# Turning the second head's chunks round in each block of v, scores and kept keys, so that the products with v address all four quarters of TensorE's array

## The chip, the cores and the metric

One core of a Trainium2 chip runs the whole kernel. The metric is the device time of one execution in microseconds (us), given as the median of several fast runs with their lowest and highest. "PEclk" in a profile is the TensorE clock that was granted, as a fraction of full speed.

## The reference, cut to what matters

A gated linear attention over 4 batches and 8 heads (768 steps, head size 48) is followed by a low-rank mixer and a feed-forward layer (384 to 1536 to 384). All in fp32.

```python
def _attn_ref(q, k, v, f_logit):            # B, H, S, D = 4, 8, 768, 48
    f = 1.0 / (1.0 + np.exp(-f_logit))
    for t in range(S):
        state = f[:, :, t, :, None] * state + np.einsum('bhd,bhe->bhde', k[:, :, t], v[:, :, t])
        y[:, :, t] = np.einsum('bhd,bhde->bhe', q[:, :, t], state)
# x = y as (B, S, H*D)
def _moe_ref(x, U, V, w_ch1, w_ch2):
    h = x.transpose(0, 2, 1) @ U @ V
    u = x + h.transpose(0, 2, 1)
    return u + np.maximum(u @ w_ch1, 0.0) @ w_ch2
```

## The kernel before

The attention goes in 16 units, each a pair of heads (`par` 0 and 1). The sequence is cut into 6 blocks of 128 steps, each of two chunks of 64 (`s` 0 and 1). Within a chunk the scores are a 64x64 triangle, and across chunks a state is carried by a scan on VectorE. A unit's work on TensorE is: kept keys (transposes), states (`ds`), scores (`sc`), products of the states with q (`y` from `st`) and products of the scores with v (`y` from `v_nat`). Between these pieces the mixer of the batch before is laid in, which is most of TensorE's work (`pz`, `pw`, `po`). For the first four units there is no mixer yet.

`part[s]` is the lower or upper 64 partitions. It is the key to the change: the partitions of the operands choose the row half of the array, and the partitions of the output choose the column half (the prediction below names the page that says so). A quarter is one row half with one column half.

```python
    # load of v: a block of 128 steps on 128 partitions, so chunk s on part[s]
    v_tiles[n] = three.tile([P, NBL, 2, D], F32, name="v_nat")
    nc.sync.dma_start(out=dst[:, :, par, 0:D], in_=head.rearrange("(c p) d -> p c d", p=P))
    # ... (cut)
        part = [slice(s * C, (s + 1) * C) for s in range(2)]          # C = 64
        def scores():       # rows: the head's half; columns: the chunk's half
            # ... loops over c (blocks), par, s
                        nc.tensor.matmul(
                            sc[part[s], par, c * C : (c + 1) * C],
                            lhsT=T["k"][rows[par], chunk[2 * c + s]],
                            rhs=T["q"][rows[par], chunk[2 * c + s]],
                            start=True, stop=True)
            # ... VectorE: A = sc * causal mask
        def kept():         # the keys turned back, chunk s on part[s]
            # ...
                    nc.tensor.transpose(pt[:, par, c * PAD : (c + 1) * PAD],
                                        T["k"][r, c * P : (c + 1) * P], ident[r, r])
        def states():       # rows: the chunk's half; columns: the head's half
            # ...
                        nc.tensor.matmul(
                            ds[par * PAD : (par + 1) * PAD, s, c * D : (c + 1) * D],
                            lhsT=T["kb"][part[s], par, c, :], rhs=vt[part[s], c, par, :],
                            start=True, stop=True)
            # ... ScalarE copies ds; a scan on VectorE gives st[e, c], chunks innermost
            T["st"] = st.rearrange("p (e c) -> p c e", c=NCH)         # NCH = 12
        def read():         # y from st: rows: the head's half; columns: the chunk's half
            # ... rhs=T["st"][rows[par], c, :]   (48 elements, 12 apart)
        def inner():        # y from v: rows AND columns are the chunk's half
            # ... loops over reversed c, par, s
                        nc.tensor.matmul(
                            o(s, par, c),                             # y[part[s], par, ...]
                            lhsT=T["A"][part[s], par, c, :], rhs=vt[part[s], c, par, :],
                            start=False, stop=True, skip_group_check=True)
```

In `inner` only the two quarters on the diagonal, (0,0) and (1,1), are ever addressed.

## Time and profile before

| | before |
|---|---|
| time, median of 3 | 548.32 us (547.5 to 548.93) |
| span of the profiled run (548.67 us) | 546.9 us |
| TensorE busy | 94% of the span |
| first product of the feed-forward layer (`pz`) starts | 72.84 us |
| from there to the end | 474.0 us |

The last two rows split the kernel into an early part (loads, conversion of weights, the first four units, the first mixer's start, with many waits) and a late part in which TensorE hardly stops. This is the clock row of the profile page, the span in 40 equal slices of 13.7 us, each digit the granted clock in tenths:

```profile
PEclk9697599999999799999999999999999999999998
```

The reader is to see the second to fifth slices (14 to 68 us) at 6, 9, 7, 5, and one 7 in the slice from 178 us. The individual clock records say that TensorE ran at exactly half clock from 18.4 to 28.6, 42.3 to 45.7 and 52.5 to 66.1 us, which is 27.3 us in all before the first `pz`.

From the chain that ended last, in order of time, these are pieces that serve as milestones (start in us, us on the chain, what):

```profile
72.84 46.86 PE pz L167 x216
...
215.66 7.97 PE pz L167 x36
...
286.32 8.00 PE pw L212 x48
...
336.27 7.97 PE pz L167 x36
...
394.23 5.38 PE pz L167 x24
...
453.66 23.58 PE pz L167 x108
...
527.85 13.66 PE pw L212 x84
```

Every one of them is TensorE's.

### The profile page before, as it was taken

Reading aid. Unit: us, or ns where it says so; the run is one execution under the profiler, and the core shown is the slowest. Engines: PE = TensorE matmul, PEld = TensorE weight load, DVE = VectorE, ACT = ScalarE, POOL = GpSimd, SP = SyncE. Lnnn points to the kernel's source line nnn. Section 1 sums busy time; section 2 is a strip of 40 time slices with the busy share of each in tenths; the row PEclk is TensorE's granted clock in tenths of the full one; section 3 lists DMA queues with packets and bytes.
Section 4 is the critical chain, followed back from the end, with each engine's and each line's share of the span. In section 5 each row is a group of like instructions: output and inputs, shape, how many; then the busy total and the mean of one; then the engine's idle time right before and its main releaser. Section 6 shows DMA issues by size and latency. Waiting matters only on the chain.

```text
span 546.9 us, 11966 instructions
## 1 busy us (share of the span) xinstructions
PE 511.6 (94%) x5277; PEld 425.3 (78%) x5277; DVE 268.7 (49%) x406; ACT 145.6 (27%) x293; POOL 33.4 (6%) x47
## 2 busy tenths in 40 slices
PE   4676889999998999999999999999999999999996
PEld 3565478886775546889889877899899877898995
DVE  5675475556666866457485740645403340222231
ACT  3243365562222113322331213221321103202010
POOL 3001243341000000000000000000000000000000
PEclk9697599999999799999999999999999999999998
DMA  9988915523546335050805522010000000000001
GB/s 149 165 163 188 225 48 159 160 80 83 106 77 88 51 65 81 1 73 12 121 3 90 71 28 44 1 24 30 2 2 31 1 16 15 1 15 15 0 30 35
DMA packets 149077, 34.88 MB, mean 64 GB/s; under 512 B 139544, under 2 KB 147224, under 8 KB 149016
## 3 DMA queue, kind: packets, MB, share of 16 engines
q1 hardware_dynamic: 149016, 34.03, 32.9%
q8 instruction: 43, 0.70, 0.6%
q14 instruction: 18, 0.15, 0.1%
HBM read 29.29 MB, written 4.72 MB: 62 GB/s over the span
## 4 chain that ended last, share of the span: by engine, by line
PE 86%; DVE 5%; SPq 2%; DMA 2%; ACT 2%; issue 1%; DVEq 0%; ACTq 0%
PE pz L167 35%; PE pw L212 23%; PE po L189 9%; PE y L613 5%; PE y L595 4%; PE pt L454 3%; SPq L359 2%; PE ds L567 2%; PE sc L534 2%; PE pu L148 1%; PE pt L553 1%; PE ph L136 1%; DMA f_raw<-in_f_logit_dram 1%; PE put L157 1%; DMA v_nat<-in_v_dram 1%
## 5 line engine op out<-in xcount | busy, mean ns | idle before, releaser
L167 PE MATMUL pz<-uT,w 128*128 128x256 f32 x864 | 192.8, 382 | 0.7 <-ACT uT L159 0.7
L167 PEld LDWEIGHTS pz<-uT,w 128*128 128x128 f32 x864 | 162.3, 190 | 23.6 <-ACT uT L159 0.6
L174 ACT ACTIVATE z<-pz 128x512 f32<-128x512 f32 x63 | 37.7, 598 | 128.5 <-PE pz L167 124.4
L212 PE MATMUL pw<-w,z 128*128 128x192 f32 x324 | 56.2, 328 | 0.0
L212 PE MATMUL pw<-zw,w_raw 128*128 128x192 f32 x324 | 56.2, 328 | 0.0
L212 PEld LDWEIGHTS pw<-w,z 128*128 128x128 f32 x324 | 53.0, 190 | 1.4 <-DVE x L144 0.5
L212 PEld LDWEIGHTS pw<-zw,w_raw 128*128 128x128 f32 x324 | 52.8, 190 | 1.5 <-DVE o L144 1.2
L144 DVE TENSOR_TENSOR w_raw<-z 128x768 f32<-128x768 f32 x18 | 17.2, 953 | 58.6 <-ACT z L174 58.5
L486 DVE TENSOR_TENSOR_SCAN X<-fz,ends 128x768 f32<-128x768 f32 x16 | 28.1, 1753 | 20.6 <-ACT fz L475 14.4
L580 DVE TENSOR_TENSOR_SCAN st<-added,whole 128x576 f32<-128x576 f32 x16 | 21.6, 1352 | 29.6 <-ACT added L573 29.6
L613 PEld LDWEIGHTS y<-v_nat,A 64*64 64x64 f32 x768 | 26.8, 149 | 5.9 <-issue 5.1
L595 PE MATMUL y<-st,qT 48*64 48x48 f32 x704 | 20.8, 271 | 10.1 <-DVE st L580 10.1
L613 PE MATMUL y<-v_nat,A 64*64 64x48 f32 x768 | 28.8, 234 | 0.5 <-ACT seen L602 0.5
L595 PEld LDWEIGHTS y<-st,qT 48*64 48x64 f32 x704 | 18.0, 164 | 14.5 <-issue 12.0
L503 DVE TENSOR_TENSOR_SCAN Y<-fz,starts 128x768 f32<-128x768 f32 x16 | 28.0, 1749 | 0.2
L68 POOL TENSOR_TENSOR w<-w_y,w_r 128x384 int32<-128x384 int32 x24 | 25.4, 1057 | 42.1 <-DVE w_y L67 40.8
L189 PE MATMUL po<-w,zw 128*128 128x384 f32 x72 | 27.2, 524 | 0.0
L189 PE MATMUL po<-w,z 128*128 128x384 f32 x72 | 25.2, 493 | 0.0
L65 DVE TENSOR_SCALAR w_y<-w_y 128x384 f32<-128x384 f32 (+1 forms) x27 | 11.1, 409 | 28.3 <-ACT w_y L63 28.3
L148 PE MATMUL pu<-h,V 128*128 128x384 f32 x48 | 21.3, 566 | 2.0 <-DVE x L144 0.7
L144 DVE TENSOR_TENSOR w_y<-x,pw 128x192 f32<-128x192 f32 x9 | 3.2, 355 | 39.3 <-ACT w_y L225 39.3
L144 DVE TENSOR_TENSOR w_y<-w_y,pw 128x192 f32<-128x192 f32 x18 | 6.3, 351 | 31.3 <-PE pw L212 31.3
(91 smaller groups left out, 510.9 us busy)
## 6 DMA issues: line engine op xcount, KB each, us to landing
w_raw<-in_moe_w_ch_dram SPq DMA_DIRECT2D x18, 384.0 KB, 3.1
v_nat<-in_v_dram SPq DMA_DIRECT2D x32, 144.0 KB, 3.5
out_dram<-o SPq DMA_DIRECT2D x24, 192.0 KB, 2.0
f_raw<-in_f_logit_dram SPq DMA_DIRECT2D x16, 144.0 KB, 2.9
k_raw<-in_k_dram SPq DMA_DIRECT2D x16, 144.0 KB, 4.2
q_raw<-in_q_dram SPq DMA_DIRECT2D x16, 144.0 KB, 4.2
zw<-in_moe_w_ch_dram SPq DMA_DIRECT2D x6, 384.0 KB, 14.5
f_raw<-in_f_logit_dram SPq DMA_DIRECT2D x16, 96.0 KB, 3.2
```

What stands on the lines that cost most here:

```text
L68: nc.gpsimd.tensor_tensor(dst.bitcast(I32), shaped(y.bitcast(I32)), shaped(r), ALU.add)
L144: nc.vector.tensor_tensor(*args)
L148: nc.tensor.matmul(pm[:, 0:DM], lhsT=V[:, t * P : (t + 1) * P], rhs=h[0], start=True, stop=True)
L167: nc.tensor.matmul(pm[:, i * 2 * P : (i + 1) * 2 * P], lhsT=w1[:, m, o : o + P], rhs=uT[a][:, m, :], start=(m == 0), stop=(m == NDC - 1))
L174: nc.scalar.activation(z[a, c][:, k : k + 2, :].rearrange("p i t -> p (i t)"), pm, AF.Relu)
L189: nc.tensor.matmul(pm, lhsT=z[a, i // NI][:, i % NI, s * P : (s + 1) * P], rhs=w2[:, i, :], start=(i == 0), stop=(i == NFC - 1))
L212: nc.tensor.matmul(pm[:, n * HM : (n + 1) * HM], lhsT=lhs[:, i, :], rhs=rhs[:, i, :], start=(i == 0), stop=(i == NI - 1))
L486: nc.vector.tensor_tensor_scan(backwards(X, S - 1, S), backwards(f, S, S), backwards(ends, S - 1, S), 0.0, ALU.mult, ALU.add,)
L503: nc.vector.tensor_tensor_scan(Y, f[:, 0:S], starts, 0.0, ALU.mult, ALU.add)
L580: nc.vector.tensor_tensor_scan(st, added[:, 0 : D * NCH], whole.rearrange("p e c -> p (e c)"), 0.0, ALU.add, ALU.mult)
L595: nc.tensor.matmul(o(c % 2, par, c // 2), lhsT=T["q"][rows[par], chunk[c]], rhs=T["st"][rows[par], c, :], start=(c <= 2), stop=False, skip ...
L613: nc.tensor.matmul(o(s, par, c), lhsT=T["A"][part[s], par, c, :], rhs=vt[part[s], c, par, :], start=False, stop=True, skip_group_check=True,)
```

## The change

The intent is to let the products with v use four quarters. For the second head (`par` 1) the two chunks of each block change places in v, in the scores and in the kept keys, while y keeps its places. So `inner` takes the operands of the second head from `part[s ^ 1]` and writes `part[s]`: quarters (1,0) and (0,1) beside the first head's (0,0) and (1,1). The states and scores keep using four quarters in another order. v's second head needs two loads of 64 partitions instead of one of 128. The kept keys of the second head are read 64 columns further left, so the key tile gets 64 zero columns in front and a fixed place. With that shift the second chunk of a block lies in the next block of kept keys, which is the `i` of `states`; the last chunk finds the zeros there, and no later chunk reads its state.

```diff
@@ load
+                if nm == "v" and par:
+                    for s in range(2):
+                        nc.sync.dma_start(
+                            out=v_tiles[n][(1 - s) * C : (2 - s) * C, :, par, :],
+                            in_=head.rearrange("(c s p) d -> s p c d", s=2, p=C)[s],
+                        )
+                    continue
@@ constants
+    kz = [const.tile([P, C + S], F32, name=f"kz{i}") for i in range(2)]
+    for i in range(2):
+        nc.gpsimd.memset(kz[i][:, 0:C], 0.0)
@@ operand
-            t = T[nm] = two.tile([P, S], F32, name=f"{nm}T")
+            t = T[nm] = kz[n % 2][:, C:] if nm == "k" else two.tile([P, S], F32, name="qT")
@@ scores
-                            sc[part[s], par, c * C : (c + 1) * C],
+                            sc[part[s ^ par], par, c * C : (c + 1) * C],
@@ kept
+                    o = c * P + (1 - par) * C
-                        pt[:, par, c * PAD : (c + 1) * PAD], T["k"][r, c * P : (c + 1) * P], ident[r, r]
+                        pt[:, par, c * PAD : (c + 1) * PAD], kz[n % 2][r, o : o + P], ident[r, r]
@@ states
+                        i = (c + (s & par)) % NBL
-                            lhsT=T["kb"][part[s], par, c, :], rhs=vt[part[s], c, par, :],
+                            lhsT=T["kb"][part[s ^ par], par, i, :], rhs=vt[part[s ^ par], c, par, :],
@@ inner
-                            o(s, par, c), lhsT=T["A"][part[s], par, c, :], rhs=vt[part[s], c, par, :],
+                            o(s, par, c), lhsT=T["A"][part[s ^ par], par, c, :], rhs=vt[part[s ^ par], c, par, :],
```

## The prediction

> **What bounds the kernel now.** I read the page's busy shares first, then the chain that ended last, then the chain piece by piece in order of time, then the groups of TensorE instructions.
>
> ```profile
> PE 511.6 (94%) x5277; PEld 425.3 (78%) x5277; DVE 268.7 (49%) x406; ACT 145.6 (27%) x293; POOL 33.4 (6%) x47
> ...
> PE 86%; DVE 5%; SPq 2%; DMA 2%; ACT 2%; issue 1%; DVEq 0%; ACTq 0%
> PE pz L167 35%; PE pw L212 23%; PE po L189 9%; PE y L613 5%; PE y L595 4%; PE pt L454 3%; SPq L359 2%; PE ds L567 2%; PE sc L534 2%; PE pu L148 1%; PE pt L553 1%; PE ph L136 1%; DMA f_raw<-in_f_logit_dram 1%; PE put L157 1%; DMA v_nat<-in_v_dram 1%
> ```
>
> The reader is to see that TensorE is busy for 94% of the span and carries 86% of the chain, so time taken off its stream is time off the end, except where something else sets the pace. The line under change, "PE y L613" (scores times v), has 5% of the chain. Going through the records for gaps in TensorE's work, I find about 25 us in all: nearly 18 us between its first instruction and 73 us, 3.5 us at 175.5 to 179.0, and the rest in pieces under 0.5 us around the mixer's additions and transposes. From 215 to 318 us there is none.
>
> Now one unit (one pair of heads) of the late part, from the chain in order of time:
>
> ```profile
> 294.31 0.84 PE ds L567 x48
> 295.16 2.15 PE pw L212 x12
> 297.31 0.86 PE sc L534 x48
> 298.17 5.38 PE pz L167 x24
> 303.54 1.17 PE y L595 x44
> 304.71 2.79 PE pz L167 x12
> 307.50 1.53 PE y L613 x48
> 309.03 4.10 PE pw L212 x24
> ```
>
> Columns: start us, us on the chain, what. Three groups have 48 instructions each on 64-column weights. The states (ds) take 0.84 us and the scores (sc) 0.86, but y L613 takes 1.53. The code says why: ds and sc touch all four quarters of the array, whereas y L613 has both its row half and its column half given by part[s], so only the two quarters on the diagonal. The groups view gives the same shapes:
>
> ```profile
> L613 PE MATMUL y<-v_nat,A 64*64 64x48 f32 x768 | 28.8, 234 | 0.5 <-ACT seen L602 0.5
> L595 PE MATMUL y<-st,qT 48*64 48x48 f32 x704 | 20.8, 271 | 10.1 <-DVE st L580 10.1
> L567 PE MATMUL ds<-v_nat,kb 64*64 64x48 f32 x768 | 14.9, 221 | 1.5 <-ACT kb L557 1.0 <-DMA v_nat<-in_v_dram 0.3
> L534 PE MATMUL sc<-qT,kT 48*64 48x64 f32 x768 | 14.5, 220 | 0.0
> ```
>
> y L613 is busy for 28.8 us, ds with the same form for 14.9. In the records one by one, ds and sc start in bursts of four, some 7 ns apart, one burst each 58 ns. y L613 starts in bursts of two, also one each 58 ns. So one quarter takes one instruction per 58 ns in all three groups, and y L613 leaves half of them empty.
>
> **What the Trainium skill says.** "TensorEngine Tiling (Array Packing)", Tile-to-Partition Mapping: in 64x64 mode there are four tiles, and rows of the operands and partitions of the output pick the tile. Its Key Properties: tiles work in parallel, and a change of tiling mode drains the engine. The trace agrees: bursts of four; and sc directly behind ds takes 0.71 us where it takes 0.86 behind a full-array product, so a switch costs about 0.15 us. The change leaves the number of switches alone. "TensorE: Matmul & The Clock Gate", LDWEIGHTS: a load takes the number of columns divided by 1.2, in ns: 53 for 64; the trace's 58 ns per instruction and quarter is near, so the weight load sets the rate of a quarter. The first page's Gotcha 1: different row tiles cannot use one PSUM bank at once. The trace doesn't show that as a loss: y L613 of before sends both row halves to one bank 7 ns apart at the full 58 ns rate. The clock page's Part 1: after idling, TensorE runs at half rate. Here the granted clock was 0.50 from 20 to 28 us and 0.68 from 54 to 73.
>
> **The change part by part.** The order of TensorE's instructions is the same in both kernels, with the same counts.
>
> Products with v (y L613): 24 products, 48 instructions, 16 units. Two quarters: 24 bursts of two, 24 x 58.3 = 1.40 us; measured from first load to last start 1.385 us. Four quarters: 12 bursts, 0.70 us, and ds with its same form measures 0.699. So 0.686 us less per unit. Late units (5th to 16th): eleven at full clock, 11 x 0.686 = 7.5; the eighth begins at half clock, 1.843 to about 0.93, 0.9 less. Sum 8.4 us. First four units: 2.50, 1.39, 1.73 and 2.50 us (two at half clock), halved: 1.2 + 0.7 + 0.9 + 1.2 = 4.0 us.
>
> States (ds): its quarters were all used, and are, in another order: now (row, column) halves (0,0), (1,1), (1,0), (0,1). No change. Scores: outputs of the second head swap halves, still four quarters, no change. Kept keys: 12 transposes of the same shape, shifted by 64 columns for the second head; no change. The key tile of fixed place stays doubled, by unit parity; no new wait.
>
> VectorE, ScalarE: the same work; from about 189 us on the scheduler orders some VectorE and ScalarE instructions otherwise. GpSimd: two 64-column clears, some 0.1 us each, behind those that the first transposes wait for.
>
> Loads: the second head of v comes in two loads of 64 partitions, 16 more issues, bytes and 192-byte packets the same. Only the start can feel it: issues are on the chain until f_raw of the third unit lands.
>
> ```profile
> 13.16 0.73 SPq L359
> 13.94 5.66 DMA f_raw<-in_f_logit_dram
> 19.60 0.14 issue
> 19.73 1.51 PE pt L454 x6
> ```
>
> Two more issues stand ahead of it (0.84 us each now), but an issue of 768 packets takes 0.84 us because the engines take packets at about 0.9 per ns: until 18 us they never run dry. Packets, not issues, set this landing; half as many per issue should take half as long. I put 0.2 us on it.
>
> What of the savings is on the path. Late: all 8.4, since the stream hardly waits; the 3.5 us gap at 175.5 starts from kept keys behind TensorE itself and moves along whole. Its VectorE order up to there is unchanged. Early: the chain in time goes through y L613 at 24.17 (2.73 us), 44.94 (1.90) and 54.23 (2.82), not through the second unit's at 34.9, where VectorE's scans lead. So 1.2 + 0.9 + 1.2 = 3.3 us, if what follows (VectorE's chain, the mixer's first products) moves up too. Sum: 8.4 + 3.3 - 0.2 = 11.5 us, and 548.3 - 11.5 = 536.8 us, 2.1% less.
>
> **The rivals.** (1) Four quarters with accumulation don't reach 58 ns. y L595 accumulates in four quarters and has a burst each 87 ns. For this: y L613 accumulates too. Against: y L595 reads st with a stride of 12 elements, its instructions are longer (median 263 ns) and y L613's have the 218 of ds. If true: 12 x 87 = 1.04 us per unit, about half the gain: 543. (2) Early gains vanish: a DMA landing or the conversions of weights set the start, so that only the late 8.4 remain: 540. For: DMA is at 80 to 99% until 30 us, and VectorE leads at 29 to 42 us. Against: after 19.7 us the chain has no landing until 65. (3) The clock: after gaps the half rate holds for some 3 to 14 us, and gaps shift; any run of it moves by 2 to 3 us either way. (4) Bank sharing slows ds, now with both row halves in one bank: ds back to 1.4 us would eat all; y L613 of before speaks against.
>
> **Range and chances.** Centre 536.8. Rival 2 and an unlucky clock give 541.5; a lucky clock and the second unit's 0.7 give 533. The line of 2% lies at 537.4, just above the centre: faster by over 2% 0.54, within 2% 0.45, slower 0.01, which needs rival 4 and worse.
>
> **What would show it.** y L613 on the chain at about 0.84 us per late unit (12 x 58 + 0.15), busy about 15 us, bursts of four. ds, sc, y L595 as now. f_raw's landing near 19.6 us. The gap of 3.5 us still there, some 5.2 us earlier. First pz product near 69.7 us instead of 72.84. Wrong: y L613 near 1.2 us (rival 1), the first pz still near 72.8 (rival 2), ds at 1.5 (rival 4), or other lengths at half clock before 73 us and around 180 (rival 3).

## The result, and the profile after

| | before | after |
|---|---|---|
| time, median of the same 4 rounds | 547.91 us (545.16 to 548.93) | 539.8 us (539.24 to 540.17) |
| ratio | | 0.9859, 95% interval 0.9821 to 0.9896 |
| span of the profiled run | 546.9 us | 537.9 us |
| first `pz` | 72.84 us | 71.26 us |
| from there to the end | 474.0 us | 466.7 us |

A ratio here and below is the mean time of one kernel's runs over the mean time of the other's runs of the same rounds, so it is not quite the ratio of the medians that are quoted. The change saves 8.1 us by the medians (9.0 in the profiled pair): 1.4%, inside the 2% line, and inside the predicted range but 3.0 us short of its centre. The results are correct.

The line numbers have shifted: the products with v are now L630 (L613), those with the states L612 (L595), states L584 (L567), scores L547 (L534), kept keys L568 (L553). The page of the changed kernel, busy shares, clock, and the chain by engine and line:

```profile
PE 504.1 (94%) x5277; PEld 416.5 (77%) x5277; DVE 268.6 (50%) x406; ACT 144.8 (27%) x293; POOL 33.5 (6%) x49
...
PEclk9875599999999799999999999999999999999999
...
PE 83%; DVE 7%; SPq 4%; ACT 2%; DMA 1%; issue 1%; DVEq 0%; ACTq 0%
PE pz L167 35%; PE pw L212 22%; PE po L189 8%; PE y L612 4%; PE pt L466 3%; PE pu L148 2%; PE y L630 2%; SPq L367 2%; SPq L373 2%; PE ds L584 2%; PE sc L547 1%; PE pt L568 1%; PE put L157 1%; PE ph L136 1%; ACT uT L159 1%
```

Three things are to be seen. The products with v (y L630) fell from 5% of the chain to 2%. TensorE's share of the chain fell from 86% to 83% while VectorE's rose from 5% to 7%. And the clock row shows two slices at 5 (40 to 67 us at a slice of 13.4 us) where before had one.

The groups of TensorE instructions (shapes kept apart), with count, busy us, mean ns and idle us before them:

```profile
L612 PE MATMUL y<-st,qT 48*64 48x48 f32 x704 | 21.2, 275 | 8.4 <-DVE st L597 8.4
...
L630 PE MATMUL y<-v_nat,A 64*64 64x48 f32 x768 | 16.5, 237 | 0.5 <-ACT seen L619 0.5
L547 PE MATMUL sc<-qT,kz 48*64 48x64 f32 x768 | 15.5, 226 | 0.9 <-issue 0.9
L584 PE MATMUL ds<-v_nat,kb 64*64 64x48 f32 x768 | 15.3, 226 | 1.2 <-ACT kb L572 0.9
```

The products with v are busy for 16.5 us instead of 28.8, with the same 768 instructions. Their neighbours moved by 0.4 to 1.0 us only, and record by record the late units' ds and y L612 are as before (698 ns and 976 to 982 ns). Their extra busy time lies in the first units, which ran more often at half clock.

A late unit in the chain in order of time:

```profile
369.64 1.17 PE y L612 x43
370.81 2.15 PE pw L212 x12
372.96 0.84 PE y L630 x48
373.80 2.79 PE pz L167 x12
```

0.84 us, where before had 1.53. The records one by one show bursts of four, 7 ns apart within a burst, and a burst each 58 ns. From first load to last start it is 699 ns a unit, and 1385 before.

The milestones of the chain, as shown of before:

```profile
71.26 46.86 PE pz L167 x216
...
211.37 7.97 PE pz L167 x36
...
279.97 8.00 PE pw L212 x48
...
330.04 7.97 PE pz L167 x36
...
386.63 5.38 PE pz L167 x24
...
444.69 23.58 PE pz L167 x108
...
518.88 13.66 PE pw L212 x84
```

Subtracted from those of before, the gain is 1.58 us at the first `pz`, 4.29, 6.35, 6.23, 7.60, 8.97 and 8.97. So the early part brought 1.6 us in this pair, not the expected 3.1. (By the medians it is less: 8.1 us in all, of which the part behind the first `pz` has 7.4, so 0.7.) From there to the second milestone four units save 3 x 0.687 + 1.145 = 3.2 us (the eighth unit began at half clock before), and the gain grows by 2.7: 0.5 us are lost. From the third to the fourth one more unit saves 0.69, and the gain goes down by 0.12: 0.8 us are lost. Elsewhere each unit brings its 0.69 in full.

Where the early gain went can be read from the same chain. The start of the second and third units' products with the states, and of the mixer's first product (`ph`), before:

```profile
32.94 1.24 PE y L595 x43
...
42.06 1.41 PE y L595 x44
...
57.86 2.79 PE ph L136 x12
```

and after:

```profile
30.95 1.52 PE y L612 x44
...
41.74 1.52 PE y L612 x44
...
56.30 2.79 PE ph L136 x12
```

The changed kernel is 1.99 us ahead at the second unit, 0.32 at the third (and 0.31 at the fourth), 1.56 at `ph`. So 1.7 us were lost inside the second unit. There the chain before runs at full clock (28.6 to 42.3 us) and through VectorE's scans, while after TensorE is at half clock from 30.7 to 37.5 us and its own products, among them the second unit's products with v (1.46 us from 33.94), have come onto the chain. The third unit gained nothing, since at half clock its kept keys (0.85 us) stepped into the place of the shortened product; the fourth gained 1.25.

The larger of the two late losses has a visible cause. The timeline of the changed kernel at the lost place (start, duration, what; in brackets the idle time before it and what ended it):

```profile
306.65 0.95 DVE L144 TENSOR_TENSOR w_raw<-z,w_raw 128x768 f32<-128x768 f32 x1
...
307.51 0.35 DVE L144 TENSOR_TENSOR w_y<-x,pw 128x192 f32<-128x192 f32 x1
...
307.89 0.35 DVE L144 TENSOR_TENSOR o<-w_y,pw 128x192 f32<-128x192 f32 x1
...
308.31 0.92 PE L212 MATMUL pw<-zw,w_raw 128*128 128x192 f32 x4 [0.80 <-DVE o L144]
```

TensorE stands for 0.80 us until VectorE has emptied the accumulators of the product before. VectorE could do that only at 307.51, when the last of four sums for the mixer (0.95 us each) was through. Those sums come after two scans of the next unit, and at this place the schedule of VectorE's instructions differs from that of before. The smaller loss, 0.50 us, lies at 196 to 201 us, where the mixer's product `po` follows `pu` behind VectorE's additions, again in another order than before.

### The profile page after: what moved, and what is told of

Its sections match the earlier page's. It is cut to its first block, busy times and chain, and to the rows that moved or that the text cites. A ratio compares the mean times of both kernels' runs of the same rounds, so it can differ in the third digit from the quotient of the medians.

```text
span 537.9 us, 11981 instructions
## 1 busy us (share of the span) xinstructions
PE 504.1 (94%) x5277; PEld 416.5 (77%) x5277; DVE 268.6 (50%) x406; ACT 144.8 (27%) x293; POOL 33.5 (6%) x49
## 4 chain that ended last, share of the span: by engine, by line
PE 83%; DVE 7%; SPq 4%; ACT 2%; DMA 1%; issue 1%; DVEq 0%; ACTq 0%
PE pz L167 35%; PE pw L212 22%; PE po L189 8%; PE y L612 4%; PE pt L466 3%; PE pu L148 2%; PE y L630 2%; SPq L367 2%; SPq L373 2%; PE ds L584 2%; PE sc L547 1%; PE pt L568 1%; PE put L157 1%; PE ph L136 1%; ACT uT L159 1%
## 5 line engine op out<-in xcount | busy, mean ns | idle before, releaser
L167 PEld LDWEIGHTS pz<-uT,w 128*128 128x128 f32 x864 | 162.3, 190 | 23.9 <-ACT uT L159 1.0
L597 DVE TENSOR_TENSOR_SCAN st<-added,whole 128x576 f32<-128x576 f32 x16 | 21.6, 1351 | 26.4 <-ACT added L590 26.4
L612 PE MATMUL y<-st,qT 48*64 48x48 f32 x704 | 21.2, 275 | 8.4 <-DVE st L597 8.4
L612 PEld LDWEIGHTS y<-st,qT 48*64 48x64 f32 x704 | 18.4, 170 | 12.8 <-issue 11.2
L189 PEld LDWEIGHTS po<-w,zw 128*128 128x128 f32 x72 | 13.8, 201 | 9.0 <-issue 1.8
L148 PEld LDWEIGHTS pu<-h,V 128*128 128x128 f32 x48 | 9.0, 210 | 13.8 <-DVE x L144 7.6
```

What stands on the lines that cost most here:

```text
L148: nc.tensor.matmul(pm[:, 0:DM], lhsT=V[:, t * P : (t + 1) * P], rhs=h[0], start=True, stop=True)
L167: nc.tensor.matmul(pm[:, i * 2 * P : (i + 1) * 2 * P], lhsT=w1[:, m, o : o + P], rhs=uT[a][:, m, :], start=(m == 0), stop=(m == NDC - 1))
L189: nc.tensor.matmul(pm, lhsT=z[a, i // NI][:, i % NI, s * P : (s + 1) * P], rhs=w2[:, i, :], start=(i == 0), stop=(i == NFC - 1))
L597: nc.vector.tensor_tensor_scan(st, added[:, 0 : D * NCH], whole.rearrange("p e c -> p (e c)"), 0.0, ALU.add, ALU.mult)
L612: nc.tensor.matmul(o(c % 2, par, c // 2), lhsT=T["q"][rows[par], chunk[c]], rhs=T["st"][rows[par], c, :], start=(c <= 2), stop=False, skip ...
```

## The experiments

The theory after the first look had three parts. The saving of the product itself is as worked out (0.69 us per late unit). The 1.3 us lost in the late part are lost because the schedule of VectorE and ScalarE came out in another order. In the early part the saved time turned into lower clock: TensorE, with less to do between the same waits, spent more time at half clock. The rivals: that the quarters or the extra loads cost something everywhere (bank sharing, issues), that the early part is bound by VectorE or by landings so that no product saved there counts, and that the order has nothing to do with the late loss.

### The loads alone

Before, with v's second head in two loads of 64 partitions, into the old places. No quarter changes.

```diff
+                if nm == "v" and par:
+                    for s in range(2):
+                        nc.sync.dma_start(
+                            out=v_tiles[n][s * C : (s + 1) * C, :, par, :],
+                            in_=head.rearrange("(c s p) d -> s p c d", s=2, p=C)[s],
+                        )
+                    continue
```

> The kernel before with one thing changed: the second head of v comes in two loads of 64 partitions, each to its old place; the products stay on two quarters. VectorE and ScalarE get the order of the changed kernel by this alone. Theory A, the other order costs: gaps of some 0.8 us ahead of a pw product near 314 us and of some 0.2 us near 200 us appear as in the changed kernel, and the time is 1 to 1.5 us over before. Theory B, the whole shortfall of the early part lies in the clock and the loads cost nothing: equal to before within 0.5 us, no such gaps. Theory C, two more issues delay the start: the first pz product over 1 us later than 72.8 us at the same stretches of half clock.

Measured: 548.75 us (546.55 to 549.36, 6 runs) beside 547.9 of before, ratio 1.0014 (0.9991 to 1.0037): the same. In the time of whole runs the extra loads cost nothing that can be measured. Compared instruction by instruction, this kernel has the VectorE and ScalarE order of the changed kernel, so the extra loads are what reorders them. The late part takes 473.5 us (before 474.0), and the 0.8 us stop is not there: with the longer products, VectorE is done in time. The other place of theory A is there, though (a stop of 0.23 us at 198.2 us). Instruction by instruction against before, this kernel loses 0.50 us there and 0.12 at 312 to 333 us; the total hides it, since its half clock behind the 3.5 us gap lasted one window of 3.4 us and not two. So the order costs about 0.6 us alone, and more together with the shorter products. Theory C is wrong: the first `pz` of the profiled run, the fastest of the six, comes at 71.22 us, with 23.9 us at half clock before it. That is as early as in the changed kernel (71.26 us with 34.1 us), without any shorter product. So the 1.6 us of one profiled pair cannot be put down to the change.

### The products with v head by head

The changed kernel with the two outer loops of the products with v exchanged, so that a head's blocks run through on its own two quarters before the other head begins.

```diff
-            for c in reversed(range(NBL)):
-                for par in range(2):
+            for par in range(2):
+                for c in reversed(range(NBL)):
```

> The changed kernel, but the products with v are given out head by head: first all 12 of one head (quarters (0,0) and (1,1) in turn), then all 12 of the other (quarters (1,0) and (0,1)). All four quarters are used, two at a time. Theory: what counts is that neighbours in the stream are in different quarters, so bursts of two each 58 ns come back: 1.39 us from first load to last start per unit at full clock, and 8 us over the changed kernel, about 548. Rival: TensorE's queue looks far enough ahead to join the two heads, or spreading data over the quarters is what counts: 0.70 us and 540.

Measured: 544.8 us (543.98 to 549.14, 5 runs), ratio 0.9934 (0.9904 to 0.9965). The same 768 instructions on the same four quarters take 1199 ns a unit, neither the 1385 of two quarters nor the 699 of four. The records show bursts of two, one each 58 ns, except from about 501 to 730 ns after the unit's first load, where the end of one head and the start of the other overlap in bursts of four. So it is not enough that four quarters occur in a group. They must alternate closely in the stream: the overlap of the two heads covered only some four bursts (0.23 us) here. The time lies between the theory (548) and its rival (540). The group of the profiled run, which is the slowest of the five (549.14 us), shows the same half way:

```profile
L630 PE MATMUL y<-v_nat,A 64*64 64x48 f32 x768 | 26.4, 241 | 0.5 <-ACT seen L619 0.5
```

26.4 us, between 28.8 and 16.5. Since this run changes nothing but the order of these products, it ties their saving to how the quarters follow one another in the stream.

### The second half of v loaded from GpSimd's queue

The changed kernel, with one of the two loads issued by GpSimd. This gives VectorE and ScalarE exactly the order they had before the change.

```diff
-                        nc.sync.dma_start(
+                        (nc.gpsimd if s else nc.sync).dma_start(
```

> The changed kernel, but the second of the two loads of v's second head is issued by GpSimd's queue. With that the scheduler gives VectorE and ScalarE exactly the order of the kernel before, and the products keep four quarters. Theory A (the order costs 1 to 1.5 us): the gap of 0.8 us ahead of pw near 308 us is gone and the time is about 538.5. Theory B (order costs nothing): 539.8 within 0.5 us, or slower if GpSimd's issues hold something up.

Measured: 537.74 us (537.03 to 538.93, 6 runs), ratio 0.9813 (0.9789 to 0.9837). The place of the 0.80 us stop, in the chain of waits of this kernel:

```profile
299.21 0.84 PE y L630 x48
300.06 4.10 PE pw L212 x24
304.15 1.41 PE ph L136 x12
305.57 4.11 PE pw L212 x24
```

TensorE passes from `ph` to the next `pw` without VectorE on the chain. From the first `pz` to the last piece of the milestones:

```profile
69.81 46.86 PE pz L167 x216
...
516.13 13.66 PE pw L212 x84
```

That is 446.32 us, where the changed kernel takes 447.62 (518.88 - 71.26) and before 455.01. So the order was worth the whole 1.3 us, and with it given back the late part saves 8.7 us, as its products do. The time to the end of the span shows only half of that (466.0 us against 466.7), because what follows TensorE's last product took 6.0 us in this run and 5.4 in before and after; that tail varies from 5.4 to 6.0 us over the twelve profiles, and why is not known. The rest of this kernel's advantage is early: its first `pz` is at 69.81 us. Its clock in the profiled run was 0.94 and 0.64 in the two early windows, the changed kernel's 0.74 and 0.62. Whether that comes from the other queue or from the luck of the clock, this run doesn't tell.

### States read as runs of 48

The prediction's first rival took the 87 ns per burst of the products with the states for a limit of accumulation. Here those products read the same memory as if it were laid out chunk by chunk, so the moving operand is contiguous. The result is wrong (relative error 0.396), and nothing else changes.

```diff
-            T["st"] = st.rearrange("p (e c) -> p c e", c=NCH)
+            T["st"] = st.rearrange("p (c e) -> p c e", c=NCH)
```

> The changed kernel, but the products of queries with states read the states as runs of 48 neighbours in place of 48 elements 12 apart. The numbers are wrong on purpose. It asks why these products take a burst each 87 ns, which my first rival put down to accumulation in four quarters. If it is the stride: a burst each 58 ns, 0.64 us from first load to last start instead of 0.98, late pieces of the chain 0.85 instead of 1.17 us, and some 5 us less in all, about 535. If it is accumulation or the 48 rows: 87 ns and 540.

Measured: 535.5 us (534.05 to 536.8, 4 runs), ratio 0.9775 (0.9742 to 0.9809). The group of TensorE instructions:

```profile
L612 PE MATMUL y<-st,qT 48*64 48x48 f32 x704 | 16.3, 237 | 8.4 <-DVE st L597 8.4
```

16.3 us busy instead of 21.2, and 685 ns a unit instead of about 978: a burst each 58 ns. These products accumulate as ever, so accumulation is no limit, and the stride of 12 elements (48 bytes) is what costs 29 ns a burst. "SBUF — State Buffer" of the Trainium skill, under the heading on the DMA port swizzle (Door 1), says that SBUF has lines of 16 bytes and that each access which crosses to a new line pays a penalty. The measurement agrees in kind, and puts a number on it for TensorE: half as long again.

### Spare products in the early part: before and after

To hold the clock, 8, 3, 5 and 4 products of 128 x 256, whose result nobody reads, stand behind the scores of the first four units. The same is done to before and to the changed kernel.

```diff
+            scores_of = scores
+            def scores_and_fill(n=n, scores_of=scores_of):
+                scores_of()
+                pm = ps_mm.tile([P, 512], F32, name="spin", tag="mm")
+                for _ in range((8, 3, 5, 4)[n]):
+                    nc.tensor.matmul(pm[:, 0:256], lhsT=ident, rhs=ends[:, 0:256], start=True, stop=True)
+            pieces[5] = scores_and_fill
```

Before with them:

> The kernel before with 8, 3, 5 and 4 spare products (128x256, read by nobody) in TensorE's stream behind the scores of the first four units, where it waits for a load or for VectorE. They are there to keep the granted clock at 1.0 up to 73 us, where it was at half rate for 27 us of it. Theory (the clock, set by these waits, decides what the start costs): little or no half clock between 20 and 73 us, first pz well ahead of 72.8 us (67 to 69), and 3 to 6 us less than before: 542 to 545. Rival: the start is led by loads and VectorE, and half clock lies beside that: first pz within 1 us of 72.8, 547 to 549.

The changed kernel with them:

> The changed kernel with the same spare products. Theory: with the clock up in both, the early saving is that of the products at full clock, on the chain for two or three units of four (0.7 each): first pz 1.4 to 2.1 us ahead of that of the kernel before with spare products; the rest as without, so some 9 us less than it (8.4 late, 1.4 to 2.1 early, less 1.4 by VectorE's order): about 533 to 536. Rival (something other than the clock eats the early saving): first pz no earlier than with spare products before.

Measured on one chip beside before at 548.15 us: before with spare products 542.99 us (542.31 to 544.89, 4 runs), ratio 0.99 (0.9885 to 0.9915); the changed kernel with them 532.25 us (531.3 to 535.29, 5 runs), ratio 0.9715 (0.9689 to 0.9742). Adding work made both kernels faster. The busy time of each engine in two windows, whose third figure from the end is the granted clock, first of before and of the changed kernel without spare products:

```profile
20.00:42.00 22.00, 17.86 (x436) 15.64 (x434) 14.68 (x18) 7.52 (x16) 0.00 (x0) 0.80 0.86 167
42.00:72.00 30.00, 23.29 (x337) 15.47 (x337) 15.43 (x31) 11.54 (x26) 6.50 (x6) 0.72 0.89 190
```

```profile
20.00:42.00 22.00, 17.44 (x445) 14.83 (x449) 15.00 (x18) 7.49 (x16) 0.00 (x0) 0.74 0.90 161
42.00:72.00 30.00, 24.34 (x344) 15.96 (x340) 15.69 (x33) 12.92 (x30) 7.52 (x7) 0.62 0.89 197
```

The clock after the change is 0.06 and 0.10 lower: 34.1 us at half clock ahead of the first `pz` instead of 27.3. With spare products, before and then the changed kernel:

```profile
20.00:42.00 22.00, 18.04 (x448) 15.49 (x449) 15.34 (x18) 7.45 (x16) 0.00 (x0) 0.97 0.84 160
42.00:72.00 30.00, 24.30 (x365) 16.80 (x364) 16.91 (x35) 14.33 (x32) 8.32 (x8) 0.97 0.91 195
```

```profile
20.00:42.00 22.00, 18.71 (x478) 15.64 (x480) 15.35 (x18) 7.42 (x16) 0.00 (x0) 1.00 0.82 155
42.00:72.00 30.00, 24.30 (x369) 17.14 (x362) 20.53 (x39) 16.57 (x37) 9.54 (x10) 1.00 0.92 197
```

Now both are near full clock, and the first `pz` comes at 69.36 and 65.83 us: 3.5 us apart, where it had been 1.6. Over whole runs the change is worth 542.99 - 532.25 = 10.7 us. Both are above what was expected (1.4 to 2.1 us, and some 9), and not all of the 3.5 us is the products'. On both chains lie the products of the second, third and fourth units, shorter by 0.67 us each, which is 2.0 us. (The first unit's is on neither: there VectorE's scans lead.) Another 2.5 us come from the third unit's spare products. TensorE stopped inside them for 3.46 us in before and for 2.43 us in the changed kernel, and behind the longer stop before fell to half clock for its one window (40.7 to 44.1 us), so that the seven spare products left took 3.15 us instead of 1.67. Against this, the changed kernel was 0.9 us behind at the second unit's products with the states. So with the clock near full the saving of the products counts early too, and the rival, that something else eats it, falls; but its size is 2.0 us and not 3.5.

### Both together, and the strided states mended

Three kernels tried to add the findings up: spare products with the GpSimd load; the same with the states copied by GpSimd into runs of 48 for the last eight units; and that copy with all loads left on SyncE.

```diff
+            if b >= TURNED:
+                rows_st = two.tile([P, D * NCH], F32, name="st")
+                rows_st = rows_st.rearrange("p (c e) -> p c e", c=NCH)
+                nc.gpsimd.tensor_copy(rows_st, T["st"])
+                T["st"] = rows_st
```

Spare products and the GpSimd load:

> The changed kernel with spare products and with the second load of v's second head issued by GpSimd, which gives VectorE the order of the kernel before. If order (1.4 us, measured 2.1 with chance in it) and clock add up: 1 to 2 us under the changed kernel with spare products. If they don't: equal to it within 0.5.

Measured: 536.75 us (535.33 to 539.72, 5 runs), ratio 0.9806 (0.9783 to 0.9829), a miss: 4.5 us slower than with all loads on SyncE. The late part is 0.8 us shorter (465.7), and 1.2 us to TensorE's last product, as the order has it. But half clock came back from 40.6 to 44.0 and from 54.2 to 57.6 us, and the first `pz` is at 67.87 us. The profiled run is the fastest of the five, so it doesn't show all of the loss.

The same with the copy of the states:

> As the last, and for the last eight units GpSimd, idle there, copies the states into runs of 48 neighbours, so that the products of queries with states go at a burst each 58 ns there, as the run with wrong numbers showed. There is 2.6 to 6.8 us of slack between the states' scan and these products. If the copy fits it: 8 x 0.29 = 2.3 us less than the last. If the copy takes longer than the slack, or disturbs VectorE: no gain or a loss.

Measured: 533.42 us (531.86 to 534.73, 5 runs), ratio 0.973 (0.9711 to 0.9749), 3.3 us less than without the copy. The products with the states take 685 ns in each of the last eight units instead of about 978; that is 8 x 0.293 = 2.3 us. What follows them on TensorE starts 0.34 us earlier each time, since the last product of a group is shorter too, and 8 x 0.34 = 2.7 us is what the late part lost (463.0 us, 2.8 less). The copies (1.2 us each) run on GpSimd, which has nothing else to do there.

Spare products, the copy, and all loads on SyncE:

> The changed kernel with spare products (8, 3, 5, 4), all loads issued by SyncE's queue, and GpSimd's copy of the states into runs of 48 for the last eight units. The version put together from what paid: the changed kernel with spare products took 532.25 us, and the copy took 2.7 us off the part behind the first pz product (466.6 to 463.9 expected), so 529.5. If the copy only paid together with VectorE's old order: 531 to 532.

Measured: 529.19 us (528.55 to 530.87, 6 runs) beside 548.12 of before, ratio 0.966 (0.9643 to 0.9677), correct, and the best version of all. It is 10.6 us below the median of the changed kernel, though that was timed in other rounds. The first `pz` is at 63.44 us and the late part takes 463.9 us.

### The best version with six spare products fewer

If the clock is what the spare products buy, then taking a few away must bring half clock back and cost time, though it removes work.

```diff
-                for _ in range((8, 3, 5, 4)[n]):
+                for _ in range((8, 3, 1, 2)[n]):
```

> The same with 8, 3, 1 and 2 spare products. In the third unit the spare products stopped half way for 2.4 us without a wait that the profile shows and held the next products up by nearly 2 us. If fewer there keep the clock up as well: 527 to 529. If the clock drops to half again in the gaps of units three and four: 530 to 534, with more half clock between 38 and 65 us.

Measured on the same chip: 533.55 us (530.71 to 534.34, 5 runs), ratio 0.9712 (0.9688 to 0.9737). Six products fewer cost 4.4 us. The window from 42 to 72 us, of the best version and then of this one:

```profile
42.00:72.00 30.00, 24.29 (x306) 17.20 (x299) 21.49 (x42) 17.82 (x39) 10.59 (x11) 1.00 0.88 196
```

```profile
42.00:72.00 30.00, 25.19 (x308) 16.59 (x305) 17.20 (x35) 14.27 (x32) 8.50 (x8) 0.68 0.97 196
```

Clock 1.00 and 0.68. The half clock lasted from 41.0 to 61.4 us, the first `pz` is at 68.96 us instead of 63.44, and the late part is the same within 0.5 us. The profiled run is the slowest of the five. This is the most direct test of the clock, and it agrees.

### When the clock falls: a count over all traces

In all traces the clock changes only on a grid of 3.41 us, which lies differently in each run. I cut the first 200 us of the twelve profiled executions along each run's own grid, and took for each window the share of time in which TensorE had a load or a product under way (windows whose clock, or whose next clock, is not on record are left out).

| window at | busy share | windows | next window |
|---|---|---|---|
| full clock | under 0.60 | 32 | 31 fall to half, 1 stays |
| full clock | 0.60 to 0.69 | 22 | 2 fall, 20 stay |
| full clock | 0.70 and over | 515 | none falls |
| half clock | 0.95 and over | 35 | 32 return to full, 3 stay |
| half clock | under 0.95 | 47 | 1 returns, 46 stay |

The one that stays is the window from 38.4 us of the changed kernel with spare products (busy share 0.53). So in these traces a window with waits of 40% or more nearly always cost the next window half its clock, and it took an almost gapless window to return. Where waits recur every few us, one fall can last long. Before and after differ in just this way. In the second unit, where the early gain went, the changed kernel had a window at 0.51 from 27.3 us, and the clock fell; before had 0.80 and 0.73 at the same work, and it stayed. At the third unit, here is a window of before, and three of the changed kernel at the same work (PE busy is the figure after the length, the clock is third from the end):

```profile
42.30:45.70 3.40, 3.40 (x66) 2.98 (x59) 1.19 (x2) 0.16 (x1) 0.00 (x0) 0.50 1.04 245
```

```profile
41.00:44.40 3.40, 2.65 (x50) 2.52 (x50) 1.45 (x2) 0.16 (x1) 0.00 (x0) 0.50 0.67 181
44.40:47.80 3.40, 2.63 (x62) 2.09 (x60) 0.96 (x1) 1.32 (x2) 0.00 (x0) 0.50 0.89 245
47.80:51.20 3.40, 2.84 (x96) 2.65 (x96) 2.83 (x7) 2.65 (x7) 0.91 (x2) 0.50 0.64 163
```

In before, products with the states, transposes and the slow products with v (1.95 us at half clock) filled one window exactly, and the clock came back at 45.7 us. In the changed kernel the same stretch is split by the grid, a wait of 0.74 us at its start and one of 0.94 us behind it fall into the two windows, and half clock lasts until 64.8 us. Both the shorter product and the place of the grid can have a part in this. Which of the two decides is not shown, since a run can't choose its grid.

### What could not be built

v's second head in one load, with the chunks turned on the DRAM side, would have kept the issues as they were: its access pattern has too many dimensions and is not accepted (it is refused for more than 3 dimensions). A scan which writes the states chunk by chunk itself, without GpSimd's copy, was refused as well, since the scan takes no operand of that many dimensions.

## Why the prediction was right or wrong

- **The product itself was right.** Twelve bursts of four, one each 58 ns; 0.84 us on the chain for a late unit, measured 0.84; 0.686 us saved, measured 0.687. The eighth unit saved 1.145 us instead of 0.9, since the clock was full again by then. Sum for the late units 11 x 0.687 + 1.145 = 8.7 us, where the prediction had 8.4. That "the weight load sets the rate of a quarter" is not shown: products with 48 and with 64 columns to move both come at 58 ns, which speaks against the moved columns, but no run varied the columns of the weights.
- **Rival 1 is false.** Products with accumulation reach 58 ns, in the changed kernel and, with a contiguous operand, in the products with the states too. The stride was the reason for 87.
- **Rival 4 is false.** The states' products take 698 to 699 ns in late units, as before.
- **The loads** were right in size: the landing of the third unit's f_raw moved from 19.60 to 19.84 us, for which the prediction had 0.2, though it named 19.6 as the time to look for. Over the runs without the extra loads it varies as much (19.60 and 19.86 us). The reason given was wrong: "half as many per issue should take half as long" did not hold, the half loads' issues before this landing took 0.86 and 0.61 to 0.64 us beside 0.84 of a whole one.
- **The gap of 3.5 us** is still there (3506 and 3507 ns), but 3.6 us earlier and not 5.2. That is the 1.6 us of the early part and three units of 0.69.
- **The step that failed is "Early: ... So 1.2 + 0.9 + 1.2 = 3.3 us, if what follows (VectorE's chain, the mixer's first products) moves up too."** The first `pz` moved up by 1.6 us instead of 3.1, and by the medians 0.7. In the profiled pair 2.0 us were gained by the start of the second unit's products with the states (the first unit's product took 0.70 us instead of 2.50, and the prediction had half; by luck of the clock it ran at half clock before and at full clock after), 1.7 of them lost again before the third unit's, nothing came in the third unit, and 1.25 in the fourth. The path was wrong at the first two units: once the first unit's product was short, the chain left it for VectorE's scans (qT from 23.99 us), and the second unit's product, which the prediction had off the path, came onto it at half clock. What the records show at the place of the 1.7 us is half clock where before had full clock, so the clock, which the prediction had as its third rival, "any run of it moves by 2 to 3 us either way", without a side, took them. That the change itself lowers the clock is not shown: the granted clock of the four timed runs of the changed kernel was 0.960 to 0.976, that of before 0.959 to 0.978, and the changed kernel's slowest run has its highest clock. With spare products in both kernels the products' part of the early gain is 2.0 us (three units of 0.67), out of 3.5.
- **"VectorE, ScalarE: the same work"** was right for the work and wrong in leaving out the order. In the profiled pair the late part gained 7.4 us (8.97 - 1.58) of the 8.7 saved, so 1.3 us are missing (the 0.5 and the 0.8 at the two places). Giving back the order brought all of it up to TensorE's last product (1.30 us, and 1.24 with spare products).
- **The sum**, for the profiled pair: 11.5 - 1.5 (early) + 0.3 (late products) - 1.3 (late waits) = 9.0 us, the difference of the spans. With spare products in both kernels it is 10.7 us, chance in the stops included. That the time fell inside the predicted range is in part luck: the late products saved 0.3 us more than predicted, which hides some of the rest. Rival 2 ("only the late 8.4 remain: 540") has the time right and the reason wrong: in the profiled pair part of the early gain was there, and part of the late gain was not.

Open points. TensorE stopped in the changed kernel inside the second unit's scores (0.88 us from 27.78 us); such a stop, of 0.12 to 0.88 us, is there in all ten profiles with the extra loads and in neither of the two without, so it goes with these loads (VectorE and ScalarE are in the order of before until 189 us). It stopped inside the spare products of before and of the changed kernel (3.46 and 2.43 us), too. None of these has a wait in the records; the cause is not known. The early gain of the GpSimd load without spare products, and its loss with them, are not explained. The share of the luck of the grid in the measured early gain can only be bounded by the spread of the runs (before: 545.16 to 549.51 us over the sessions).

## What to carry to other kernels

Count which quarters each group of small products addresses, and whether they alternate closely in the stream; a group whose operand half and output half are tied to the same index uses half the array, and turning the data round for every other head doubles its rate. A saving before a wait can be lost to the clock, as 1.7 us were here: where TensorE waits often, look at the clock row before and after, and try a few spare products, since they can be worth more than the saving. Also compare the order of the other engines' instructions, because an extra load can reschedule them (1.3 us here). And take more than one profile before a gain of 1 or 2 us in such a stretch is put down to the change.

## What the Trainium skill lacked or had wrong

- "TensorE: Matmul & The Clock Gate", Why this matters for your kernels, asks for no idle gaps over some 3 us between bursts. That row alone is not strict enough here: the clock fell behind windows whose longest stop was 0.82, 0.94, 1.04 and 1.13 us. What counted was the sum of stops in a window: 31 of 32 windows busy for under 60% were followed by half clock, and none of 515 busy for 70% or more.
- The same page, Part 1, gives a free-running window of 3413 ns and says that one busy window brings the clock back. The traces agree on the grid of 3.41 us, and on one window, and they add the numbers: 32 of 33 returns came after windows busy for 95% or more, and at 0.66 to 0.83 half clock lasted for 24 us on end. The page gives no thresholds.
- The same page, Part 3, What overlaps and what doesn't, has weight loads overlap products in flight only where the row group differs. In these traces loads to two quarters of the same row half start 7 to 20 ns apart and overlap products of the same rows, and the rate is one load per quarter in 58 ns.
- The same page's part on the queue speaks of a partial reorder window of 64 instructions. When the two pairs of quarters came one after the other, the overlap covered only about 0.23 us, some four bursts (1199 ns a unit instead of 699).
- "SBUF — State Buffer" names the penalty for crossing lines of 16 bytes, but no page gives its size for a moving operand of TensorE in fp32: at a stride of 48 bytes a burst took 87 ns instead of 58, 978 ns a unit instead of 685.
- "TensorEngine Tiling (Array Packing)", Gotcha 1, says that row tiles cannot use one PSUM bank at once. No run here shows a loss: products of both row halves into one bank start 7 ns apart at 58 ns a burst.
